# Segmented attention beside a gated MLP: filler of the score groups with three gate buffers, rings for K copies and Q chunks, and target periods

## The chip, the cores and the metric

The kernel runs on one core of one Trainium2 chip. The time is the device time of one launch in microseconds (us); all inputs and outputs lie in device memory. TensorE (PE) multiplies matrices into PSUM, VectorE (DVE) and ScalarE (ACT) read PSUM and SBUF, GpSimd (POOL) here only masks, SyncE (SP) issues DMAs.

## The reference

Both halves read the same x of shape 1 x 2048 x 512 in bf16. The first half is attention with a memory: 32 heads of width 16, the sequence cut into four segments of 512 rows.

```python
for s in range(4):
    logits = einsum('bhqd,bhkd->bhqk', qs, ks) * scale + mask     # causal inside the segment
    a_dot  = einsum('bhqk,bhkd->bhqd', softmax(logits), vs)
    a_mem  = (phi(qs) @ M) / (phi(qs) @ z + 1e-6)                 # phi(t) = t+1 for t>0, else exp(t)
    o      = g * a_mem + (1 - g) * a_dot                          # g = sigmoid(beta), one per head
    M, z   = M + phi(ks)^T vs, z + sum(phi(ks))
a = o @ wo
b = (gelu(x @ w_gate) * (x @ w_up)) @ w_down                      # 512 -> 1792 -> 512
out = sg * a + (1 - sg) * b                                       # sg = sigmoid(x . gate_w)
```

## The kernel before

All inputs are loaded once by SP in an order written by hand, and everything stays in SBUF. The x of each segment is held transposed (`xT`). The instruction order on every engine is written out by the program itself, at build time, by a small planner.

**Score groups.** The spine is a loop over four segments `s`, in each over four chunks `c` of eight heads, in each over five groups A to E: 80 groups in all, numbered by `clock`. `group_qk` writes the scores of one group into the single four-bank PSUM tile `lg` and ACT takes the exponential of it (`pT`). One group later `pv` multiplies the masked result by V (`od`). `finish` normalises on DVE (`rden`, `o2`). For s > 0 `mem_num` multiplies phi(q) by the memory (`mn`) and DVE scales it by `rdm`, which `u_den` computes. A finished chunk is transposed by a DMA into `oT` two groups later (`tr_o`).

**Filler.** Between a group's scores and its PV, PE is filled with units: `u_k`, `u_q`, `u_v` (projections of the next segment), `u_gate`, `u_up`, `u_down` (the MLP), `u_out` (the output), `u_M`, `u_den` (the memory). A projection, gate, up or output unit is four 512-wide matmuls into one of three general PSUM banks (`gen`) and one copy or product on DVE. `u_k` has two masked copies more, `KT`, for even and odd heads; `u_down` has 14 matmuls. Each unit carries an estimate of its PE and DVE time.

**Choice.** Units stand in streams, each in its own order: P (all projections and memory of one segment), G (gates), U (ups, then downs), O (outputs). `fill_to(t)` issues units until PE's planned time reaches `t`. It takes the first stream that has a unit allowed. If the planned backlog of DVE is over 0.5 us and the projections are not late against a linear pace, it takes the unit with the least DVE time per PE time:

```python
if backlog[0] > 0.5 and not late:
    st = min(hs, key=lambda x: x.q[0][1] / x.q[0][0])
start(st)
```

The feature maps phi (`u_phq`, `u_phk`) are issued by `later(lag, ...)`, some groups after their chunk. `u_absmax_x` and `u_bound` compute a bound on the scores that decides at the end whether a general path (not taken here) must run. The gate activations of a segment are copied to `G[s % 2]` and go through two large GELUs on ACT (`gelu`); for segment 0 ACT takes them straight out of PSUM in the opening.

**Buffers.** `G`, `QT` and `KTm` have two buffers each, taken by the segment's parity, so the gates of segment s wait for all downs of segment s-2, and all projections of a segment must be done before its first group.

Of the kernel before, what the change touches and what calls it, by code (L numbers as in the profile page):

```python
# [11 lines left out]
ALU = mybir.AluOpType  # L12
# [10 lines left out]
EXP_LIMIT = 80.0  # L23
BF = dt.bfloat16
# [11 lines left out]
TAIL_FILL = 5.5  # L36


@with_exitstack
def kernel(  # L40
# [188 lines left out]
    def u_q(s, c):  # L229
        def f():  # L230
            T = gen("qT")
            for fc in range(FC):
                nc.tensor.matmul(T[:, :], lhsT=wq[:, fc, c * P:(c + 1) * P],  # L233
                                 rhs=xT[:, fc, s * L:(s + 1) * L],
                                 start=(fc == 0), stop=(fc == FC - 1))
                if fc < FC - 1:
                    yield MM512
            nc.vector.tensor_copy(QT[s % 2][:, c, :], T[:, :])  # L238
            return MM512
        return 4 * MM512, EVAC, f  # L240
# [33 lines left out]
    def u_phq(s, c):  # L274
        def f():
            phi(pq[s % 2][:, c:c + 2, :], QT[s % 2][:, c:c + 2, :], ("q", s, c), 2 + c // 2)
        return 0.0, 0.0, f

    def u_phk(s, c):
        def f():  # L280
            phi(phk[:, c:c + 2, :], ktb[:, c:c + 2, :], ("k", s, c), 1 + c // 2)
        return 0.0, 0.0, f

    def u_k(s, c):
        def f():
            T = gen("kT")
            for fc in range(FC):
                nc.tensor.matmul(T[:, :], lhsT=wk[:, fc, c * P:(c + 1) * P],  # L288
                                 rhs=xT[:, fc, s * L:(s + 1) * L],
                                 start=(fc == 0), stop=(fc == FC - 1))  # L290
                if fc < FC - 1:
                    yield MM512
            nc.vector.tensor_copy(ktb[:, c, :], T[:, :])  # L293
            for p in range(2):
                nc.vector.tensor_scalar(out=KTm[s % 2][p][:, c, :], in0=ktb[:, c, :],  # L295
                                        scalar1=eo[:, p:p + 1], scalar2=None, op0=ALU.mult)
            return MM512
        return 4 * MM512, EVAC + 0.6, f
# [51 lines left out]
    def u_gate(s, hs, direct):  # L350
        def f():
            T = gen("gT")
            for fc in range(FC):
                nc.tensor.matmul(T[:, :], lhsT=wga[:, fc, hs * P:(hs + 1) * P],  # L354
                                 rhs=xT[:, fc, s * L:(s + 1) * L],
                                 start=(fc == 0), stop=(fc == FC - 1))
                if fc < FC - 1:
                    yield MM512
            if direct:
                nc.scalar.activation(G[s % 2][:, hs, :], T[:, :], AF.Gelu_apprx_tanh)  # L360
            else:
                nc.vector.tensor_copy(G[s % 2][:, hs, :], T[:, :])  # L362
            return MM512
        return 4 * MM512, EVAC, f

    def gelu(s):
        for h0 in range(0, HS, 7):
            g = G[s % 2][:, h0:h0 + 7, :]
            nc.scalar.activation(g, g, AF.Gelu_apprx_tanh)  # L369

    def u_up(s, hs):
        def f():
            T = gen("uT")
            for fc in range(FC):
                nc.tensor.matmul(T[:, :], lhsT=wup[:, fc, hs * P:(hs + 1) * P],  # L375
                                 rhs=xT[:, fc, s * L:(s + 1) * L],
                                 start=(fc == 0), stop=(fc == FC - 1))
                if fc < FC - 1:
                    yield MM512
            g = G[s % 2][:, hs, :]  # L380
            nc.vector.tensor_tensor(out=g, in0=T[:, :], in1=g, op=ALU.mult)  # L381
            return MM512
        return 4 * MM512, EVAC, f
# [3 lines left out]
    def u_down(s, qt):  # L387
        def f():
            T = gen("dT")
            for hs in range(HS):  # L390
                nc.tensor.matmul(T[:, :], lhsT=G[s % 2][:, hs, qt * P:(qt + 1) * P],  # L391
# [67 lines left out]
    def u_den(s):  # L459
        def f():  # L460
            assert ("q", s, 0) in ready and ("q", s, 2) in ready
            T = gen("zd")
            Tv = T[:, 0:KT * H].rearrange("p (q h) -> p q h", q=KT)
            for c in range(NC8):
                for qq in range(KT):
                    nc.tensor.matmul(Tv[:, qq, 8 * c:8 * c + 8],
                                     lhsT=pq[s % 2][:, c, qq * P:(qq + 1) * P],
                                     rhs=Mz[s % 2][:, c, :], start=True, stop=True)
                if c < NC8 - 1:
                    yield 0.12  # L470
            r = rdm[s % 2]
            nc.vector.tensor_scalar_add(r[:, :, :], Tv, 1e-6)
            nc.vector.reciprocal(r[:, :, :], r[:, :, :])
            nc.vector.tensor_tensor(out=r[:, :, :], in0=r[:, :, :],
                                    in1=gh[:, None, :].to_broadcast((P, KT, H)), op=ALU.mult)
            return 0.12
        return 0.5, 0.8, f
# [3 lines left out]
    def mem_num(s, c):  # L481
        assert count(("Mn", s)) > c // 2
# [13 lines left out]
    def group_qk(s, c, g):  # L496
# [8 lines left out]
        for pp, kt, off in pieces:  # L505
            n = L - kt * P
            for j in range(4):
                nc.tensor.matmul(lg[:, j, off:off + n],  # L508
                                 lhsT=KTm[s % 2][pp][32 * j:32 * j + 32, c, kt * P:(kt + 1) * P],
                                 rhs=QT[s % 2][32 * j:32 * j + 32, c, kt * P:L],  # L510
# [60 lines left out]

    class Stream:
        def __init__(self, name, units):
            self.name, self.q = name, deque(units)
            self.total = sum(u[0] for u in units)

    def unit(u, key=None, when=None):
        return u + (key, when)
# [55 lines left out]
    def fill_to(t):  # L634
        while True:
# [28 lines left out]
    for c in range(NC8):  # L664
        run(u_k(0, c))
# [5 lines left out]
    run(u_phk(0, 0))  # L671
    run(u_phk(0, 2))
# [19 lines left out]

    for s in range(NSEG - 1):
        us = []
        if True:
            now = (lambda s=s: clock[0] >= 20 * s + 2)
            us += [unit(u_pk(s, c), None,
                        lambda s=s, c=c: ("k", s, c - c % 2) in ready and clock[0] >= 20 * s + 2)
                   for c in range(NC8)]
            for c in range(NC8):  # L700
                us += [unit(u_k(s + 1, c), None, now), unit(u_q(s + 1, c))]
                if c % 2 == 1:
                    if s + 1 < NSEG - 1:
                        us.append(unit(u_phk(s + 1, c - 1)))
                    us.append(unit(u_phq(s + 1, c - 1)))
            us += [unit(u_v(s + 1, kt)) for kt in range(KT)]
            us += [unit(u_M(s, half)) for half in range(2)]
            us += [unit(u_mask(s + 1))]
            us.append(unit(u_den(s + 1), ("proj", s + 1),
                           lambda s=s: ("q", s + 1, 0) in ready and ("q", s + 1, 2) in ready))  # L710
            if s == 0:
                for i in range(NSEG):
                    us.insert(3 + 5 * i, unit(u_gate_logits(i)))
                us.insert(14, unit(u_absmax_x(2)))
                us.insert(19, unit(u_absmax_x(3)))
            if s == 1:
                us.insert(4, unit(u_bound()))
            streams.append(Stream("P", us))

    us = []  # L720
    for s in range(1, NSEG):
        us += [unit(u_gate(s, hs, False), None,
                    (lambda s=s: s < 2 or count(("down", s - 2)) == KT)) for hs in range(HS)]
        us.append(unit(u_gelu(s)))
    streams.append(Stream("G", us))

    us = []
    for s in range(NSEG):
        us += [unit(u_up(s, hs), None, lambda s=s: s == 0 or count(("gelu", s)) == 1)
               for hs in range(HS)]  # L730
        for qt in range(KT):
            us.append(unit(u_down(s, qt), ("down", s),
                           lambda s=s, qt=qt: count("gate") == 1
                           and (s == 0 or count(("out", s - 1)) > qt)))
# [44 lines left out]
    for s in range(NSEG):  # L779
        oT = wk2.tile([P, FC, L], BF, name="oT", tag="oT")  # L780
        oTs[s] = oT
        assert s == 0 or count(("proj", s)) == 1
        for c in range(NC8):
            for g in "ABCDE":
                clock[0] += 1
                t = group_qk(s, c, g)
# [51 lines left out]
    def general_blocks(s, c, p, tiles):  # L838
        spare = G[(s + 1) % 2]
# [5 lines left out]
        for qq in range(KT):  # L845
            n = (qq + 1) * P
            lg = plg.tile([P, 4, 512], F32, name="lg", tag="lg")
            for j in range(4):
                nc.tensor.matmul(lg[:, j, 0:n], lhsT=QT[s % 2][:, c, qq * P:n],
# [20 lines left out]
    def general():  # L870
# [3 lines left out]
        for s in range(NSEG):  # L874
# [7 lines left out]
            if s > 0:  # L882
                for c in range(0, NC8, 2):
                    phi_now(pq[s % 2][:, c:c + 2, :], QT[s % 2][:, c:c + 2, :])
                run(u_mask(s))
                run(u_den(s))
            neg = G[(s + 1) % 2][:, 8, 0:P]
# [70 lines left out]
```

## Time and profile before

| | us |
|---|---|
| median of three runs (297.51 to 299.5) | 299.48 |
| profiled execution | 299.61 |
| its span | 297.9 |
| PE busy | 280.0 (94%) |
| DVE busy | 214.1 (72%) |
| ACT busy | 200.8 (67%) |
| POOL busy | 83.4 (28%) |

The profile is of one execution. Times in its views count from the start of the span; what is beside the span in the run's time is 1.7 us. A line such as `PE gT L354 <- DVE QT L238: 2.2, 1, 2.2` says that PE, ahead of an instruction of line 354 that writes `gT`, sat idle until an instruction of DVE that writes `QT` was done: the sum in us, how often, and the longest. Rows of groups give the instruction's line, engine, operation, output and inputs, shapes and count, then its busy time, the mean of one in ns, and the idle time before. A matmul's duration includes its way through the array, so matmuls that follow each other overlap.

### The profile page before, as it was taken

To read this page: it belongs to the slowest core of one execution; us is meant where nothing else is said; L and a number is where in the kernel's file an instruction comes from. 1 tells how busy PE (TensorE), PEld (TensorE's weight loads), DVE (VectorE), ACT (ScalarE), POOL (GpSimd) and SP (SyncE) were. 2 spreads that over 40 slices of the span, in tenths; PEclk is the share of its full clock that TensorE was granted. 3 is DMA by queue.
4 is the path that set the end of the run, shared out by engine and by line. 5 is a ranking of instruction groups with operands and counts; after the bars stand their busy time and mean duration, and the time that the engine had idled before them with its cause. 6 is when DMAs were issued, how large, how long until landed. Compare 5 with 4: busy or idle time off the path is not lost. (4 is left out here: it accounts for less than half of the span.)

```text
span 297.9 us, 6858 instructions
## 1 busy us (share of the span) xinstructions
PE 280.0 (94%) x2910; PEld 138.4 (46%) x2960; DVE 214.1 (72%) x413; ACT 200.8 (67%) x125; POOL 83.4 (28%) x140
## 2 busy tenths in 40 slices
PE   7999999899999986999989999999999999999993
PEld 4444355454444443445445444455454454544551
DVE  1988698989945778678895396887886455775453
ACT  3236978698957768379976668677698666766600
POOL 4000134212243333130224433433401434244400
PEclk9999999999999999799999999999999999999998
DMA  6999850000023100000002141000000101001012
GB/s 215 319 266 212 294 74 20 0 2 20 0 20 72 21 2 19 2 10 10 0 2 55 28 80 37 3 18 2 20 0 19 36 20 37 0 21 37 21 39 77
DMA packets 29445, 15.86 MB, mean 53 GB/s; under 512 B 21984, under 2 KB 28384, under 8 KB 29408
## 3 DMA queue, kind: packets, MB, share of 16 engines
q1 hardware_dynamic: 29408, 15.35, 20.6%
q8 instruction: 25, 0.41, 0.6%
q14 instruction: 12, 0.10, 0.1%
HBM read 8.14 MB, written 2.10 MB: 34 GB/s over the span
## 5 line engine op out<-in xcount | busy, mean ns | idle before, releaser
L513 ACT ACTIVATE pT<-lg 128x2048 bf16<-128x2048 f32 x80 | 150.1, 1877 | 62.1 <-PE lg L508 52.2
L524 POOL TENSOR_SCALAR_AFFINE_SELECT pT<-pT 128x512 bf16<-128x512 bf16 x128 | 80.2, 644 | 198.9 <-ACT pT L513 197.0
L354 PE MATMUL gT<-xT,wga 128*128 128x512 bf16 x216 | 55.6, 388 | 4.7 <-DVE QT L238 2.2
L391 PE MATMUL dT<-wdn,G 128*128 128x512 bf16 x213 | 55.1, 380 | 0.9 <-issue 0.5
L375 PE MATMUL uT<-xT,wup 128*128 128x512 bf16 x211 | 51.9, 379 | 1.6 <-DVE G L381 0.8
L534 PEld LDWEIGHTS <-pT 128*128 128x128 bf16 x1280 | 43.6, 96 | 19.7 <-issue 2.6
L534 PE MATMUL od<-V,pT 128*128 128x17 bf16 x1280 | 44.0, 170 | 0.6 <-DVE o L544 0.4
L381 DVE TENSOR_TENSOR G<-uT,G 128x512 bf16<-128x512 f32 x56 | 37.7, 688 | 7.9 <-PE uT L375 7.8
L362 DVE CAST G<-gT 128x512 bf16<-128x512 f32 x42 | 28.0, 686 | 7.8 <-PE gT L354 7.2
L508 PE MATMUL lg<-QT,KT 32*128 32x384 bf16 (+3 forms) x512 | 31.7, 301 | 1.7 <-issue 1.1
L354 PEld LDWEIGHTS <-wga 128*128 128x128 bf16 x224 | 19.9, 98 | 27.9 <-issue 10.4
L375 PEld LDWEIGHTS <-wup 128*128 128x128 bf16 x224 | 19.5, 97 | 22.3 <-issue 3.9
L391 PEld LDWEIGHTS <-G 128*128 128x128 bf16 x224 | 18.5, 97 | 20.6 <-issue 5.0
L396 DVE TENSOR_SCALAR tB<-dT,omg 128x512 bf16<-128x512 f32 x16 | 12.0, 749 | 20.5 <-PE dT L391 20.4
L540 DVE RECIPROCAL rden<-od 128x16 f32<-128x16 f32 x32 | 8.2, 256 | 25.6 <-PE od L534 25.6
L508 PEld LDWEIGHTS <-KT 32*128 32x128 bf16 x512 | 9.0, 92 | 30.1 <-issue 29.6
L369 ACT ACTIVATE G<-G 128x3584 bf16<-128x3584 bf16 x6 | 18.8, 3182 | 0.0
L233 PE MATMUL qT<-xT,wq 128*128 128x512 bf16 x57 | 16.5, 380 | 0.8 <-DVE QT L238 0.2
L288 PE MATMUL kT<-xT,wk 128*128 128x512 bf16 x62 | 15.8, 379 | 0.6 <-issue 0.3
L360 ACT ACTIVATE G<-gT 128x512 bf16<-128x512 f32 x14 | 8.4, 598 | 11.3 <-PE gT L354 11.3
L408 PE MATMUL aT<-wo,oT 128*128 128x512 bf16 x58 | 15.6, 379 | 0.4 <-issue 0.2
L310 PE MATMUL vT<-wv,xT 128*128 128x512 bf16 x61 | 15.1, 379 | 0.1
(81 smaller groups left out, 222.8 us busy)
## 6 DMA issues: line engine op xcount, KB each, us to landing
out_dram<-osb SPq DMA_DIRECT2D x16, 128.0 KB, 1.7
wga<-in_B_w_gate_dram SPq DMA_DIRECT2D x1, 1792.0 KB, 12.4
wup<-in_B_w_up_dram SPq DMA_DIRECT2D x1, 1792.0 KB, 7.9
wdn<-in_B_w_down_dram SPq DMA_DIRECT2D x1, 1792.0 KB, 8.9
G<-in_A_x_dram SPq DMA_DIRECT2D x1, 512.0 KB, 4.1
wk<-in_A_wk_dram SPq DMA_DIRECT2D x1, 512.0 KB, 5.1
wq<-in_A_wq_dram SPq DMA_DIRECT2D x1, 512.0 KB, 5.9
wv<-in_A_wv_dram SPq DMA_DIRECT2D x1, 512.0 KB, 8.4
```

What stands on the lines that cost most here:

```text
L233: nc.tensor.matmul(T[:, :], lhsT=wq[:, fc, c * P:(c + 1) * P], rhs=xT[:, fc, s * L:(s + 1) * L], start=(fc == 0), stop=(fc == FC - 1))
L288: nc.tensor.matmul(T[:, :], lhsT=wk[:, fc, c * P:(c + 1) * P], rhs=xT[:, fc, s * L:(s + 1) * L], start=(fc == 0), stop=(fc == FC - 1))
L354: nc.tensor.matmul(T[:, :], lhsT=wga[:, fc, hs * P:(hs + 1) * P], rhs=xT[:, fc, s * L:(s + 1) * L], start=(fc == 0), stop=(fc == FC - 1))
L362: nc.vector.tensor_copy(G[s % 2][:, hs, :], T[:, :])
L369: nc.scalar.activation(g, g, AF.Gelu_apprx_tanh)
L375: nc.tensor.matmul(T[:, :], lhsT=wup[:, fc, hs * P:(hs + 1) * P], rhs=xT[:, fc, s * L:(s + 1) * L], start=(fc == 0), stop=(fc == FC - 1))
L381: nc.vector.tensor_tensor(out=g, in0=T[:, :], in1=g, op=ALU.mult)
L391: nc.tensor.matmul(T[:, :], lhsT=G[s % 2][:, hs, qt * P:(qt + 1) * P], rhs=wdn[:, hs, :], start=(hs == 0), stop=(hs == HS - 1))
L508: nc.tensor.matmul(lg[:, j, off:off + n], lhsT=KTm[s % 2][pp][32 * j:32 * j + 32, c, kt * P:(kt + 1) * P], rhs=QT[s % 2][32 * j:32 * j + 3 ...
L513: nc.scalar.activation(pT[:, :, :], lg[:, :, :], AF.Exp, scale=DH ** -0.5)
L524: nc.gpsimd.affine_select(out=v, in_=v, pattern=pat, compare_op=ALU.is_ge, fill=0.0, base=0, channel_multiplier=-1)
L534: nc.tensor.matmul(od[:, qq, j, 0:17], lhsT=t[:, j, o:o + P], rhs=V[s % 2][:, kt, 8 * c + 2 * j + p, 0:17], start=(kt == 0), stop=(kt == qq))
```

## The change

- `G` has three buffers, `G[s % 3]`: gates of segment s wait for the downs of segment s-3.
- `QT` has one buffer, in which a chunk is overwritten after its last score group. `KTm` is a ring of three chunks. So K and Q chunks of all segments form one sequence each, and a chunk may be issued once its place is free (`clock >= ...`).
- The opening computes three K chunks instead of four; the fourth is filler. The feature maps of k are filler from the start.
- The streams are eight instead of P, G, U, O: K, Q, V, M (transposes of phi(k), memory sums, denominators), Z (small parts), G, U, D (downs), O. Each unit has a target period `want`, a number of a group.
- `fill_to` takes the unit with the least target, where the target is shifted by DVE's backlog times the unit's DVE time per PE time.
- `need` issues what a group cannot do without, if it has not been issued.
- `u_den` is done for two chunks at a time, so its three small DVE operations run twice on half the width.
- The lags of the feature maps are the same for all chunks.

```diff
+NG = 3
+NK = 3
+WEIGH = 5.0
...
-    G = [const([P, HS, L], BF, f"G{i}") for i in range(2)]
-    QT = [const([P, NC8, L], BF, f"QT{i}") for i in range(2)]
-    KTm = [[const([P, NC8, L], BF, f"KT{p}{i}") for p in range(2)] for i in range(2)]
+    G = [const([P, HS, L], BF, f"G{i}") for i in range(NG)]
+    QT = const([P, NC8, L], BF, "QT")
+    KTm = [const([P, NK, L], BF, f"KT{p}") for p in range(2)]
...
-                nc.vector.tensor_scalar(out=KTm[s % 2][p][:, c, :], in0=ktb[:, c, :],
+                nc.vector.tensor_scalar(out=KTm[p][:, (NC8 * s + c) % NK, :], in0=ktb[:, c, :],
...
-    def u_den(s):
+    def u_den(s, pair):
...
-            for c in range(NC8):
+            for cc in range(2):
+                c = 2 * pair + cc
...
+            h0 = 16 * pair
+            r = rdm[s % 2][:, :, h0:h0 + 16]
+            nc.vector.tensor_scalar_add(r, Tv, 1e-6)
+            nc.vector.reciprocal(r, r)
...
-            st = hs[0]
-            if st.name == "P":
-                pace = st.total * (1.0 - ((clock[0] - 1) % 20) / 16.0)
-                late = sum(u[0] for u in st.q) > pace and backlog[0] < 1.5
-            else:
-                late = False
-            if backlog[0] > 0.5 and not late:
-                st = min(hs, key=lambda x: x.q[0][1] / x.q[0][0])
+            st = min(hs, key=lambda x: x.q[0][5] + WEIGH * x.q[0][1] / x.q[0][0] *
+                     (backlog[0] - 0.8))
             start(st)
...
-    for c in range(NC8):
+    for c in range(NK):
         run(u_k(0, c))
...
+    for i in range(NK, NSEG * NC8):
+        s, c = i // NC8, i % NC8
+        us.append(unit(u_k(s, c), 5 * i - 9, ("k", s),
+                       lambda i=i, s=s, c=c: clock[0] >= 5 * (i - NK) + 5 and
+                       (s == 0 or ("k", s - 1, c - c % 2) in ready)))
...
+    for i in range(NC8, NSEG * NC8):
+        s, c = i // NC8, i % NC8
+        us.append(unit(u_q(s, c), 5 * i - 11, ("q", s),
+                       lambda i=i: clock[0] >= 5 * (i - NC8) + 5))
...
+        us += [unit(u_v(s, kt), 20 * s - 13 + 3 * kt, ("v", s),
+                    lambda s=s: clock[0] >= 20 * s - 18) for kt in range(KT)]
...
+        us += [unit(u_M(s, half), 20 * s + 15) for half in range(2)]
+        us.append(unit(u_mask(s + 1), 0))
+        us += [unit(u_den(s + 1, pair), 20 * s + 18 + 10 * pair, ("den", s + 1),
+                    lambda s=s, pair=pair: ("q", s + 1, 2 * pair) in ready)
+               for pair in range(2)]
...
+    us = [unit(u_gate_logits(i), 3 + 3 * i) for i in range(NSEG)]
+    us += [unit(u_absmax_x(2), 14, None, lambda: clock[0] >= 14),
+           unit(u_absmax_x(3), 18, None, lambda: clock[0] >= 18),
+           unit(u_bound(), 45, None, lambda: clock[0] >= 45)]
...
+        us += [unit(u_gate(s, hs, False), 20 * (s - 1) + 1.1 * hs, None,
+                    lambda s=s: s < NG or count(("down", s - NG)) == KT) for hs in range(HS)]
...
+        step_ = 1.2 if s < NSEG - 1 else 0.6
+        us += [unit(u_up(s, hs), 20 * s + 1 + step_ * hs, ("up", s),
+                    lambda s=s: s == 0 or count(("gelu", s)) == 1) for hs in range(HS)]
...
+        first, step_ = ((18, 5), (38, 5), (58, 3), (70, 2.5))[s]
+        us += [unit(u_down(s, qt), first + step_ * qt, ("down", s),
...
-        us += [unit(u_out(s, qt), ("out", s),
+        us += [unit(u_out(s, qt), 20 * s + 24 + 4 * qt, ("out", s),
                     lambda s=s, qt=qt: count(("down", s)) > qt and count(("tr", s)) == NC8)
...
+    def need(key, n):
+        while count(key) < n:
+            if current:
+                step()
+            else:
+                heads()
+                start([st for st in streams if any(u[3] == key for u in st.q)][0])
```

More of the change, by code (lines that the diff above doesn't have):

```diff
@@ L280, in f @@
         def f():
-            phi(phk[:, c:c + 2, :], ktb[:, c:c + 2, :], ("k", s, c), 1 + c // 2)
+            phi(phk[:, c:c + 2, :], ktb[:, c:c + 2, :], ("k", s, c), 1)
         return 0.0, 0.0, f
@@ L574, in __init__, with unit @@
             self.name, self.q = name, deque(units)
-            self.total = sum(u[0] for u in units)
-    def unit(u, key=None, when=None):
-        return u + (key, when)
+    def unit(u, want, key=None, when=None):
+        return u + (key, when, want)
     streams = []
@@ L690, in u_gelu @@
         return 0.0, 0.0, f
[L693 to L718, printed above, removed]
@@ new lines, in free @@
+    def free(i):
+        return lambda: clock[0] >= 5 * (i - NK) + 5
+    us = [unit(u_phk(0, 0), 0)]
+    for i in range(NK, NSEG * NC8):
[3 more added lines that the diff above has]
+                       (s == 0 or ("k", s - 1, c - c % 2) in ready)))
+        if c % 2 == 1 and s < NSEG - 1:
+            us.append(unit(u_phk(s, c - 1), 0, None,
+                           lambda s=s: s == 0 or count(("pk", s - 1)) == NC8))
```

89 lines of the change are left out of this document (52 added, 37 removed).

## The prediction

> **What bounds the kernel now.** I read the page first (shares, clock row), then the waits summed by pair, then the time in stretches of 10 us, then the timeline at the worst stretch.
>
> ```profile
> PE 280.0 (94%) x2910; PEld 138.4 (46%) x2960; DVE 214.1 (72%) x413; ACT 200.8 (67%) x125; POOL 83.4 (28%) x140
> PEclk9999999999999999799999999999999999999998
> ACT pT L513 <- PE lg L508: 52.2, 54, 4.7
> PE gT L354 <- DVE QT L238: 2.2, 1, 2.2
> PE gT L354 <- DVE G L362: 1.0, 2, 0.8
> PE gT L354 <- DVE tm L489: 0.9, 1, 0.9
> PE uT L375 <- DVE G L381: 0.8, 1, 0.8
> PE od L534 <- DVE o L544: 0.4, 1, 0.4
> PE qT L233 <- DVE QT L238: 0.2, 1, 0.2
> PE qT L233 <- DVE ktb L293: 0.2, 1, 0.2
> ```
>
> TensorE (PE) sets the end: ScalarE (ACT) waits 52.2 us for it, and what PE itself waits for is nearly always VectorE (DVE). In the loop over the 80 score groups these waits are 2.2 + 1.0 + 0.9 + 0.8 + 0.4 = 5.3 us in six places, and 0.4 us more stand in the opening projections. The place matters:
>
> ```profile
> 100.00:110.00 10.00, 8.93 (x99) 4.34 (x100) 9.01 (x20) 6.76 (x4) 4.00 (x7) 1.00 0.07 15
> 110.00:120.00 10.00, 7.66 (x84) 3.52 (x83) 8.18 (x18) 7.41 (x5) 3.42 (x6) 0.94 0.07 14
> 120.00:130.00 10.00, 9.66 (x94) 4.46 (x94) 7.11 (x13) 4.82 (x3) 1.86 (x3) 0.89 0.01 2
> 230.00:240.00 10.00, 9.68 (x137) 5.07 (x135) 4.69 (x11) 6.71 (x5) 3.71 (x6) 1.00 0.14 38
> 115.36:118.77 3.41, 1.23 (x14) 0.44 (x12) 3.25 (x9) 2.96 (x3) 1.38 (x3) 1.00 0.20 41
> 118.77:122.18 3.41, 3.41 (x16) 1.31 (x16) 2.73 (x5) 0.00 (x0) 1.06 (x2) 0.50 0.00 0
> 116.16 0.40 PE L508 MATMUL lg<-QT,KT 32*128 32x256 bf16 x8
> 117.39 0.69 DVE L267 TENSOR_TENSOR phk<-phe,pha 128x1024 bf16<-128x1024 bf16 x1
> 118.00 0.68 DVE L238 CAST QT<-qT 128x512 bf16<-128x512 f32 x1
> 118.73 2.72 PE L354 MATMUL gT<-xT,wga 128*128 128x512 bf16 x6 [2.18 <-DVE QT L238]
> ```
>
> Columns of the stretches: length, busy time of PE, PEld, DVE, ACT, POOL, granted clock, DMA share, GB/s. Where projections, their copies and gate copies come together (100 to 130 us) DVE is 7 to 9 us busy of 10 and PE loses time; at 230 to 240 DVE has 4.69 us and PE runs through. At 116 us PE has nothing to do for 2.18 us because the copy of a Q chunk stands behind the feature map (L267) in DVE's order and all three general PSUM banks are full. Directly behind it the clock is 0.50 for 3.41 us, which costs 3.41 x 0.5 = 1.7 us.
>
> **The change, part by part.** PE's work is the same: the same number of matmuls of each kind stands in both programs. One K chunk (four matmuls) moves from the opening into the loop, which shifts 0.87 us and adds nothing. What changes is the order of the filler between score groups, so I count what each of the 80 groups issues in either program and multiply by these rows:
>
> ```profile
> 281.27 3.04 PE dT L391 x14
> 180.22 0.89 PE od L534 x36
> 193.68 0.25 PE MT L428 x4
> 156.81 0.33 PE lg L508 x8
> L381 DVE TENSOR_TENSOR G<-uT,G 128x512 bf16<-128x512 f32 x56 | 37.7, 688 | 7.9 <-PE uT L375 7.8
> L295 DVE TENSOR_SCALAR KT<-ktb,eo 128x512 bf16<-128x512 bf16 x32 | 12.2, 424 | 0.6
> L396 DVE TENSOR_SCALAR tB<-dT,omg 128x512 bf16<-128x512 f32 x16 | 12.0, 749 | 20.5 <-PE dT L391 20.4
> L540 DVE RECIPROCAL rden<-od 128x16 f32<-128x16 f32 x32 | 8.2, 256 | 25.6 <-PE od L534 25.6
> L541 DVE TENSOR_TENSOR rden<-rden,og 128x16 f32<-128x16 f32 x32 | 10.4, 325 | 1.1
> L544 DVE TENSOR_TENSOR o<-od,rden 128x256 bf16<-128x256 f32 x32 | 13.6, 424 | 1.1
> L762 DVE TENSOR_TENSOR o<-o,tm 128x512 bf16<-128x512 bf16 x12 | 5.1, 425 | 0.4
> L473 DVE RECIPROCAL rdm<-rdm 128x128 f32<-128x128 f32 x3 | 2.9, 953 | 0.1
> L206 DVE TENSOR_REDUCE bound<-bT x1: 534/534/534, 108.8 to 108.8; 1x3 f32<-1x384 f32 x1
> ```
>
> A 512-wide matmul is 3.04/14 = 0.217 us, a PV matmul 0.025, an M matmul 0.062, a group's scores 0.33. So a projection or gate unit is 0.87 us of PE and 0.69 of DVE, a K unit 0.69 + 2 x 0.42 = 1.54 of DVE, a down unit 3.04 of PE and 0.75 of DVE. The running sum "DVE work minus PE time, never below nothing" over the groups shows how far DVE is behind. With three banks, of which one is being written, PE can run two units ahead, 1.7 us.
>
> Before: in groups 7 to 10 DVE gets 13.9 us against 10.9 of PE, in 25 to 32 24.2 against 21.1. The sum is over 1.5 us in 17 of 80 groups, with 4.0 the highest; the waits above lie in or at the start of these stretches (51 to 55 us is group 8, 116 us group 28, 147 to 151 us group 35). After: Q and K chunks come one at a time over the whole segment and gate and up units are paired evenly; the sum is over 1.5 us in 5 groups (50 to 53, highest 2.3, where the three tiny tests of the bound, each as dear as the 0.53 us of the L206 row, meet a K chunk and a feature map; and 63 with 1.7), and 1.4 in group 20. So most of the stalls should go, not all: by the size of the present ones I keep 0.8 us at group 52 and 0.4 at 20 and 63, 1.6 us; bounds 0 and 4.2 (rivals below).
>
> The six waits of the loop are 5.3 us idle. A matmul counts as busy for 0.38 us though the next may start after 0.217, so each stall is 0.16 us longer than its idle time: 5.3 + 6 x 0.16 = 6.3 us. The slow clock goes with the 2.2 us stall: 1.7 us. The shorter opening (three K chunks, 1.5 us less DVE work ahead of the Q copies) takes its 0.4 us.
>
> The half clock is weighed against a rule by itself. The Trainium skill, "TensorE: Matmul & The Clock Gate", section on HAM oscillation, puts the fall to half rate at idle gaps over some 3.4 us; here 2.18 us of idle, in a stretch with 1.23 us busy of 3.41, preceded it. By the page that stall would be too short and the slow stretch would stay; by the row it goes. The result with it is the fourth case below.
>
> Three edits are costed at next to nothing. The third G buffer lets the gate of the next segment but one start early; no transfer or PE work is added. The division of `u_den` into two pairs turns three small operations into six of half size: between nothing and twice the 0.95 us of the reciprocal and its neighbours (0.28 and 0.29 us by their groups, not shown), I take 0.3 us of DVE per segment, which the running sum has in it. QT without a second buffer and KT as a ring of three make new chunks wait for old score matmuls; these stand ahead of the chunk's own matmuls on PE, and every copy is issued at least three groups, some 8 us, ahead of its first reader, so nothing is late. Up units now begin in group 1, at about 32 us; their weights are there:
>
> ```profile
> 16.30 0.51 SPq L114 DMA_DIRECT2D wup<-in_B_w_up_dram  x1
> 30.23 0.39 PE L508 MATMUL lg<-QT,KT 32*128 32x512 bf16 x4
> wup<-in_B_w_up_dram SPq DMA_DIRECT2D x1, 1792.0 KB, 7.9
> DMA to landing us min/median/max: 2.4/2.4/4.4
> ```
>
> 16.3 + 7.9 = 24.2 us. One step adds a wait. `u_out` has its own stream and target periods, and segment 0's first output unit now stands in group 23, close behind the transpose of that segment's last chunk (before: 16 groups after the segment's end; segments 1 and 2 keep five and nine groups in between). After the last PV matmul, in group 21, DVE has 0.6 to 1.1 us of K copies to end and 0.26 + 0.33 + 0.42 = 1.0 for the chunk; the transpose lands 2.4 later: 4.0 to 4.5 in all. PE has cover until the output unit's fourth matmul, the one that reads this chunk: 15 512-wide matmuls (3.3), two score groups (0.66), 4 PV (0.1), 4.0 us. So PE waits 0 to 0.5 us, up to 1.1 if already the unit's first matmul waits; all filler behind it waits too. I take 0.4.
>
> Sum against the profiled execution, 299.6 us (span 297.9 and 1.7 around it; the runs' median is 299.5, so nothing is to be converted): 299.6 - 6.3 - 1.7 - 0.4 + 1.6 + 0.4 = 293.2 us.
>
> **The rivals.**
>
> Cleaner than that: no stall is left at groups 20, 52 and 63, and the transpose is in time: 293.2 - 1.6 - 0.4 = 291.2. For it speaks that sums of 2.4 to 3.0 at groups 9 and 10 brought no listed wait; against it that group 45 with 1.0 did (the 0.4 us for `o`). ACT sets no bound close by: its waits for `lg` and for POOL's mask come to
>
> ```profile
> ACT pT L513 <- POOL pT L524: 9.7, 12, 1.1
> 104.44 1.88 ACT L513 ACTIVATE pT<-lg 128x2048 bf16<-128x2048 f32 x1 [0.64 <-PE lg L508]
> ```
>
> 61.9 us in 66 places; with 0.64 in each, what a prompt group shows, they would be 42, so ACT could end nearly 20 us sooner.
>
> The change does not do what it says: the picker weighs only the units' own copies, while feature maps, normalisations and bound tests fall on DVE by the clock of groups. Then two thirds of the 6.3 us stay, in new places (4.2 instead of 1.6), and with one wait near 2 us a slow stretch as well: 293.2 + 2.6 + 1.7 = 297.5. For it: DVE's work is the same to 2%. Against: the count by groups.
>
> The slow stretch stays for a reason of its own, the page's rule: 293.2 + 1.7 = 294.9.
>
> Slower: DVE becomes the bound of the whole stretch in which projections run. In groups 1 to 63 of the changed kernel it gets 165.7 us of work for 185.6 of PE, 0.89, with hardly a group in which it could catch up, and it must wait for each unit's last matmul before it can copy. If it works only 0.83 of the time there (8.18 of 10 us at 110 to 120 in the kernel before), the stretch takes 165.7 / 0.83 = 199.6: 14.0 more, in place of the 1.6 kept, 305.6. It decides from a share under 0.89 on, and makes the kernel slower by 1% at 165.7 / 196.5 = 0.84. Against it:
>
> ```profile
> 70.00:80.00 10.00, 9.79 (x101) 4.45 (x102) 9.36 (x20) 8.55 (x8) 3.71 (x6) 1.00 0.01 2
> ```
>
> where DVE is busy 9.36 of 10 us and PE hardly loses any.
>
> **How the numbers follow.** Forecast 293.2: 0.50, with 291.3 to 295.3 as its own spread. Cleaner, 291.2: 0.15. Slow stretch stays, 294.9: 0.10. Two thirds of the stalls stay, 297.5: 0.15. DVE as the bound, 305.6: 0.07. Something else slower: 0.03. Faster by over 1%, about what a measurement of this kernel can tell from no change (its runs spread by 0.7%), means below 296.5: the first three and 0.02 of the fourth, 0.77. Within 1%: 0.14. Slower: 0.09. The range goes from the cleaner case with the opening another microsecond better, 290.0, to a little over the fourth case, 298.3; outside lie DVE as the bound and the tails.
>
> **What would show it.** Right: the waits of PE for DVE in the loop sum to 1 to 2 us with none over 1; no stretch at clock 0.50 between 6 us and the end of the matmuls; DVE in the 10 us stretches up to 230 us between 6.5 and 9.2; the first score matmul near 29 us and the span near 291.5; a short wait of PE `aT` for the transpose at about 95 us. Wrong: PE stalls of 1 us or more for QT, KT or `tm` copies, `lg` waiting for KT or QT, up units waiting for their weights at 32 us, or ACT's waits for `lg` shrunk to 0.64 each while PE waits for ACT.

## The result, and the profile after

The changed kernel took 295.71 us (295.11 to 296.18, four runs) beside 298.5 of the kernel before (297.39 to 299.5, four runs): ratio 0.9893, 95% interval 0.9849 to 0.9938, 2.8 us or 1.1% faster. The forecast was 293.2 with 290.0 to 298.3.

One thing must be known to read any ratio below: the kernel before took 299.1 to 300.3 us at a mean granted clock of 0.991 to 0.994 in 36 of the 58 runs that later experiments shared, and 297.4 to 298.1 us at 0.996 to 1.0 in the other 22. The profiled execution, 299.61 us, is one of the 36 and shows what sets them apart: the stretch at clock 0.50. All four runs of the changed kernel had 0.997 to 0.999. Against the 22, some 297.7, the change is worth 2.0 us, and the ranges do not touch.

The page and the waits of the changed kernel (profiled execution 295.11, span 293.3):

```profile
PE 283.3 (97%) x2960; PEld 138.3 (47%) x2960; DVE 215.6 (74%) x422; ACT 200.8 (68%) x125; POOL 83.4 (28%) x140
PEclk9999999999999999999999999999999999999999
ACT pT L525 <- PE lg L519: 45.2, 49, 2.4
PE dT L397 <- DVE G L387: 1.3, 2, 1.1
PE uT L381 <- DVE G L387: 1.0, 1, 1.0
PE uT L381 <- DVE G L368: 0.2, 1, 0.2
```

The 5.3 us of the loop's six waits for VectorE (DVE) have become 2.5, and two waits, 1.1 and 1.0, hold most of that. The clock row has no dip, and ScalarE (ACT) still waits 45.2 us for the scores, so TensorE (PE) still sets the end. PE's busy totals are not to be compared: of PE's 2960 matmuls the trace of before holds 2910. Stretches of 10 us:

```profile
70.00:80.00 10.00, 8.90 (x96) 4.76 (x94) 7.59 (x17) 9.36 (x6) 1.86 (x3) 1.00 0.06 13
100.00:110.00 10.00, 9.86 (x102) 4.52 (x95) 7.58 (x13) 7.01 (x5) 3.96 (x7) 1.00 0.05 16
110.00:120.00 10.00, 10.00 (x145) 5.44 (x144) 9.44 (x22) 7.50 (x6) 3.71 (x6) 1.00 0.22 50
120.00:130.00 10.00, 10.00 (x111) 4.65 (x109) 7.31 (x14) 7.39 (x4) 3.30 (x6) 1.00 0.24 46
140.00:150.00 10.00, 9.21 (x103) 4.84 (x102) 8.15 (x19) 8.47 (x6) 3.08 (x5) 1.00 0.06 13
230.00:240.00 10.00, 10.00 (x99) 4.94 (x98) 7.63 (x14) 7.84 (x5) 1.85 (x3) 1.00 0.01 2
```

From 110 to 120 us, where PE had lost most, it now loses nothing, with DVE busier than before (9.44 of 10 us). The loss sits at 70 to 80 and at 140 to 150. The timeline at the first place:

```profile
73.33 0.42 DVE L556 TENSOR_TENSOR o<-od,rden 128x256 bf16<-128x256 f32 x1
73.47 1.03 PE L316 MATMUL vT<-wv,xT 128*128 128x512 bf16 x4
73.67 0.68 DVE L185 TENSOR_REDUCE amax<-xT 128x1 f32<-128x512 bf16 x1
74.26 0.42 DVE L271 TENSOR_SCALAR pha<-QT 128x1024 bf16<-128x1024 bf16 x1
74.34 1.03 PE L381 MATMUL uT<-xT,wup 128*128 128x512 bf16 x4
74.79 0.69 DVE L273 TENSOR_TENSOR pq<-phe,pha 128x1024 bf16<-128x1024 bf16 x1
74.82 6.27 ACT L375 ACTIVATE G<-G 128x3584 bf16<-128x3584 bf16 x2
75.40 0.42 DVE L446 TENSOR_TENSOR Mn<-Macc,bm 128x256 bf16<-128x256 f32 x1
75.73 0.68 DVE L387 TENSOR_TENSOR G<-uT,G 128x512 bf16<-128x512 f32 x1
76.47 1.89 PE L397 MATMUL dT<-wdn,G 128*128 128x512 bf16 x8 [1.10 <-DVE G L387]
```

Here ACT is taken by the large GELU (6.27 us), so the planner puts a long row of filler between two score groups. In front of it DVE has five small operations (o, amax, pha, pq, Mn) ahead of the product that frees a PSUM bank (75.73); the banks are full and PE stands still for 1.10 us. At 148.8 us the second GELU does the same with another set of small operations.

Where the span's 4.6 us came from, by the first and last PE rows of each part:

| | before | after | difference |
|---|---|---|---|
| first K matmul | 6.93 | 6.20 | -0.73 |
| to the first score matmul | 23.30 | 22.05 | -1.25 |
| to the last chunk's transpose on PE | 257.62 | 254.39 | -3.23 |
| to the end of the span | 10.03 | 10.67 | +0.64 |

The K chunk moved 0.87 us from the second row into the third, and three matmuls of a down unit (0.65) from the third into the fourth. Without moved work the opening became 0.4 us shorter and the loop 3.45, of which 1.7 is the half-clock stretch; the other 1.75 is put down to waits. The first row can't be put down to the change: in the profiles of the experiments, most with this same opening, the first K matmul starts anywhere from 6.13 to 7.08 us, so two runs can differ by almost 1 us before the first K chunk. In experiments 1, 2 and 5 the opening also waited 0.8 to 1.8 us for the DMA of `wq`; where it did not, it took 22.05 to 22.07 us with three K chunks and 23.30 to 23.32 with four.

### The profile page after: what moved, and what is told of

Read it like the earlier page. It is cut to its first block, busy times and chain, and to the rows that moved or that the text cites. A ratio compares the mean times of both kernels' runs of the same rounds, so it can differ in the third digit from the quotient of the medians.

```text
span 293.3 us, 6911 instructions
## 1 busy us (share of the span) xinstructions
PE 283.3 (97%) x2960; PEld 138.3 (47%) x2960; DVE 215.6 (74%) x422; ACT 200.8 (68%) x125; POOL 83.4 (28%) x140
## 4 chain that ended last, share of the span: by engine, by line
PE 86%; DVE 11%; issue 1%; ACT 1%; DVEq 0%
PE dT L397 17%; PE gT L360 16%; PE uT L381 16%; PE od L546 10%; PE lg L519 8%; PE kT L294 4%; PE vT L316 4%; PE aT L414 4%; PE qT L239 4%; DVE ktb L299 1%; PE warm L147 1%; DVE tm L500 1%; DVE KT L301 1%; DVE rden L553 1%; DVE o L556 1%
## 5 line engine op out<-in xcount | busy, mean ns | idle before, releaser
L525 ACT ACTIVATE pT<-lg 128x2048 bf16<-128x2048 f32 x80 | 150.1, 1876 | 59.7 <-PE lg L519 45.2
L381 PE MATMUL uT<-xT,wup 128*128 128x512 bf16 x224 | 62.2, 380 | 1.4 <-DVE G L387 1.0
L360 PE MATMUL gT<-xT,wga 128*128 128x512 bf16 x224 | 59.3, 379 | 0.4
L368 DVE CAST G<-gT 128x512 bf16<-128x512 f32 x42 | 28.8, 686 | 6.6 <-PE gT L360 6.3
L397 PEld LDWEIGHTS <-G 128*128 128x128 bf16 x224 | 19.8, 97 | 24.0 <-issue 4.8
L239 PE MATMUL qT<-xT,wq 128*128 128x512 bf16 x64 | 17.1, 378 | 0.2
L294 PE MATMUL kT<-xT,wk 128*128 128x512 bf16 x64 | 17.3, 379 | 0.1
L316 PE MATMUL vT<-wv,xT 128*128 128x512 bf16 x64 | 17.0, 380 | 0.0
L414 PE MATMUL aT<-wo,oT 128*128 128x512 bf16 x64 | 16.3, 380 | 0.0
L299 DVE CAST ktb<-kT 128x512 bf16<-128x512 f32 x16 | 11.0, 690 | 5.3 <-PE kT L294 5.1
```

The lines of the kernel that those rows point to most:

```text
L316: nc.tensor.matmul(T[:, :], lhsT=xT[:, fc, s * L + kt * P:s * L + (kt + 1) * P], rhs=wv[:, fc, :], start=(fc == 0), stop=(fc == FC - 1))
L368: nc.vector.tensor_copy(G[s % NG][:, hs, :], T[:, :])
L397: nc.tensor.matmul(T[:, :], lhsT=G[s % NG][:, hs, qt * P:(qt + 1) * P], rhs=wdn[:, hs, :], start=(hs == 0), stop=(hs == HS - 1))
L525: nc.scalar.activation(pT[:, :, :], lg[:, :, :], AF.Exp, scale=DH ** -0.5)
```

## The experiments

"Full clock" means a run without the half-clock stretch. All medians stand beside runs of the kernel before on the same chip, whose medians were 299.35 to 299.58.

**1. The stall at 116 us, and the half clock.** The kernel before, with the bound test one segment later:

```diff
-            if s == 1:
+            if s == 2:
                 us.insert(4, unit(u_bound()))
```

> The kernel before, with the three tests of the bound (`u_bound`) issued among the projections of segment 3 instead of segment 2, nothing else. Theory (the stall of 2.2 us at 116 us comes from DVE being late, and the stretch at clock 0.50 behind it comes from that stall): the stall falls under 1 us, no stretch at clock 0.50 stands before the end of the matmuls, and the time is 299.5 - 2 - 1.7 = 295.8 us, 295.3 to 297. Rival (the slow stretch has a cause of its own, as the Trainium skill's rule of 3.4 us of idleness would have it): the stall goes, a slow stretch stays, 297.5.

297.89 us (297.33 to 298.09, ten runs), ratio 0.9958 (0.9934 to 0.9983). The clock was 0.996 to 1.0 in all ten, where 36 of 58 runs of the kernel before have the stretch. The time forecast by the theory, 295.8, was missed. The 2.2 us wait is gone, but the waits came up elsewhere:

```profile
PE gT L354 <- DVE G L362: 1.7, 2, 0.9
PE gT L354 <- DVE QT L238: 0.7, 1, 0.7
PE MT L428 <- DVE V L314: 0.6, 1, 0.6
PE uT L375 <- DVE G L362: 0.5, 1, 0.5
PE uT L375 <- DVE tm L489: 0.4, 1, 0.4
PE od L534 <- DVE o L544: 0.4, 1, 0.4
```

So the half clock goes when the one long stall goes. The stall's own 2.2 us did not go: the time is that of the kernel before at full clock, and the loop, 255.8 us, is before's 257.6 less the 1.7 of the stretch.

**2. The third gate buffer**, in the changed kernel: `NG = 2` instead of 3.

> The changed kernel with two gate buffers instead of three, so gates of segment s again wait for the downs of segment s-2. Theory (the gain is the spreading of DVE work by targets and backlog, for which the third buffer is hardly needed): the running sum of DVE work against PE time stays under 1.6 us in all groups, and the time is 295.0 to 296.5 against 295.7 of the changed kernel. Rival (the gates that run ahead in the third buffer are what keeps PE fed): 297.5 or more, with PE waits at the segment ends.

295.49 us (295.21 to 296.37, four runs), ratio 0.9887 (0.9834 to 0.9939). The waits at the two GELUs are still 1.1 and 1.0. The theory holds: the third buffer is worth nothing that can be measured.

**3. The picker's weight**, in the changed kernel: `WEIGH = 0.0` instead of 5.0, so that target periods alone decide between the streams (nine of them: K, Q, V, M, Z, G, U, D, O).

> The changed kernel with WEIGH = 0: units are picked by their target periods alone, DVE's backlog has no say. The running sum is then over 1.5 us in 13 groups (18 to 28, 49, 50) instead of 5. Theory (the shift by backlog is a part of the gain): 1.5 to 3 us of PE waits for DVE more, 297 to 299. Rival (targets alone spread the work, the weight is idle): 295.7 within 0.5.

302.04 us (301.77 to 302.12, four runs), ratio 1.0106 (1.0053 to 1.0159): 6.3 us slower than with the weight, slower than before, and 3 us more than the theory's upper end. The clock row, and the timeline where it falls:

```profile
PEclk9999999999989999999999999999999999999999
84.23 0.40 PE L519 MATMUL lg<-QT,KT 32*128 32x256 bf16 x8
84.34 0.69 DVE L368 CAST G<-gT 128x512 bf16<-128x512 f32 x1 [0.17 <-PE gT L360]
84.95 0.68 DVE L185 TENSOR_REDUCE amax<-xT 128x1 f32<-128x512 bf16 x1
85.54 0.42 DVE L271 TENSOR_SCALAR pha<-QT 128x1024 bf16<-128x1024 bf16 x1
86.06 0.69 DVE L273 TENSOR_TENSOR pq<-phe,pha 128x1024 bf16<-128x1024 bf16 x1
86.81 0.35 PE L473 MATMUL zd<-Mz,pq 128*128 128x8 bf16 x8 [2.18 <-DVE pq L273]
84.13:87.54 3.41, 1.23 (x20) 0.61 (x20) 2.99 (x8) 3.41 (x3) 1.86 (x3) 1.00 0.00 0
87.54:90.95 3.41, 3.41 (x20) 1.09 (x18) 3.01 (x6) 0.03 (x1) 0.63 (x2) 0.50 0.00 0
```

Again a stall of 2.18 us, by another wait in another place, PE busy 1.23 us in the 3.41 around it, and behind it 3.41 us at clock 0.50, which is 1.7 of the 6.3 us. All four runs had 0.992 or 0.993.

**4. Absolute maxima and bound test moved** to groups 64 to 78, where no projections run:

```diff
-    us += [unit(u_absmax_x(2), 14, None, lambda: clock[0] >= 14),
-           unit(u_absmax_x(3), 18, None, lambda: clock[0] >= 18),
-           unit(u_bound(), 45, None, lambda: clock[0] >= 45)]
+    us += [unit(u_absmax_x(2), 64, None, lambda: clock[0] >= 64),
+           unit(u_absmax_x(3), 68, None, lambda: clock[0] >= 68),
+           unit(u_bound(), 73, None, lambda: clock[0] >= 73)]
```

> The changed kernel with the eight absmax reductions of x (0.68 us of DVE each, groups 15 to 22) and the bound tests (group 45 on) moved to groups 64 to 78, where DVE has little to do. Theory (the 1.1 us wait of PE for G at 76 us, and the one at 150 us, come from small DVE work issued ahead of the bank-freeing copies at the start of the GELU groups 17 and 40): the wait at group 17 loses some 0.7 us, the one at group 40 stays, and 294.6 to 295.4. Rival (these waits are set by something else, the ups' order): 295.7 and the same two waits of 1.1 and 1.0.

294.79 us (294.53 to 295.91, four runs), ratio 0.9879 (0.9823 to 0.9934). The wait at the first GELU, where an amax stood in DVE's row, falls from 1.10 to 0.55; at the second, where none stood, it stays, as the theory has it. The medians differ by 0.9 us, but the ranges overlap, so the two waits say more than the time:

```profile
76.56 1.02 PE L381 MATMUL uT<-xT,wup 128*128 128x512 bf16 x4 [0.55 <-DVE Macc L440]
149.86 1.02 PE L381 MATMUL uT<-xT,wup 128*128 128x512 bf16 x4 [1.04 <-DVE G L387]
```

**5. Up units closer together**: the kernel of experiment 4 with one up unit every 1.1 groups instead of 1.2.

> The kernel of e4_absmax_late with the ups' target step 1.1 instead of 1.2, so that at the GELU groups all ups of the segment are done and a down unit (14 matmuls, one DVE operation) can stand first. Theory (the two waits at the start of the GELU groups come from up and V units whose copies queue behind 3.6 us of small DVE work there): both waits fall under 0.3 us and the time is 1.0 to 1.5 us under that of e4_absmax_late, 293.3 to 294.0. Rival (DVE is late there whatever the units' order, the wait only moves to the next unit): 294.8 within 0.4.

293.87 us (292.79 to 294.19, six runs), ratio 0.9817 (0.9779 to 0.9854). The time is as the theory has it. Of the two waits, none is left at the second GELU, but 0.6 us stays near the first, and a new one of 1.0 us stands at 260.7 (`uT` for `osb`).

**6. Only the shorter opening**, on the kernel before with its own picker and buffers:

```diff
-    for c in range(NC8):
+    for c in range(NC8 - 1):
         run(u_k(0, c))
...
-    run(u_phk(0, 2))
...
             if s == 0:
+                us = [unit(u_k(0, 3)), unit(u_phk(0, 2))] + us
```

> The kernel before with one part of the change alone: three K chunks in the opening, the fourth (with its feature map) as the first filler. Theory (the opening loses one K unit's 0.87 us, which the loop gets, and 0.4 us of waits): the first score matmul comes 1.2 us earlier, and the time is 0.4 us under that of the kernel before at the same clock. Rival (the 1.5 us of DVE work that moves into groups 1 to 16, where the running sum is highest, comes back as PE waits): first score matmul 1.2 us earlier, time equal or up to 1 us longer.

295.82 us (295.45 to 296.01, six runs), ratio 0.9891 (0.9854 to 0.9927), which is the time of the whole change, and full clock in all six. This was not expected by either theory. The opening itself gave the 0.4 us again. The rest came in the loop, where the longest waits are 1.0 and 0.9 us, and experiments 8, 9 and 11 ask whether it belongs to the edit.

**7. The weight as well**: experiment 4 with an up unit every 1.15 groups and `WEIGH = 4.0`.

> The kernel of e4_absmax_late with the ups' step 1.15 and WEIGH 4, which by the order of instructions puts the GELU one group ahead of the Q feature map and of the masking of the memory in segments 0 and 1, so that the GELU groups 17 and 40 get 7.6 and 8.5 us of DVE work instead of 10.4 and 12.0, but still begin with up and V units. Theory (it is the small DVE work at the start of these groups that makes the waits): both waits fall under 0.4 us as in e5_ups_earlier, 293.5 to 294.2. Rival (only a unit without copies at the start helps): one or both waits of 1 us stay, 294.8.

292.31 us (291.72 to 293.04, six runs), ratio 0.9776 (0.9739 to 0.9814). It beats both kernels and lies below what its theory forecast (293.5); as two settings changed at once, no run divides the gain between them. All waits of PE for DVE in the loop that its trace lists, and the stretches that were worst before:

```profile
PE gT L360 <- DVE G L368: 0.4, 1, 0.4
PE qT L239 <- DVE QT L244: 0.2, 1, 0.2
100.00:110.00 10.00, 10.00 (x134) 5.16 (x133) 6.84 (x13) 7.67 (x5) 3.67 (x6) 1.00 0.05 15
110.00:120.00 10.00, 10.00 (x110) 4.92 (x111) 9.67 (x22) 8.15 (x5) 3.15 (x6) 1.00 0.35 76
120.00:130.00 10.00, 10.00 (x113) 4.66 (x112) 7.83 (x15) 7.00 (x5) 4.29 (x7) 1.00 0.18 31
```

(The `qT` wait is in the opening.) DVE is busy 9.67 of 10 us and PE loses nothing.

**8. Four K chunks in the opening**, in the changed kernel with two gate buffers: `NK = 4`, and both feature maps of k first in the filler.

```diff
-    us = [unit(u_phk(0, 0), 0)]
+    us = [unit(u_phk(0, 0), 0), unit(u_phk(0, 2), 0)]
```

> The changed kernel with four K chunks in the opening, as before the change; to have room, G has two buffers (which cost nothing in e2_two_G) and the K ring four chunks. Theory A (the parts add: the shorter opening is worth 1.2 us, of which the moved unit gives 0.87 back): 295.7 + 0.4 = 296.1, first score matmul at 29.5 to 30.3 us. Theory B (e6_three_K_before shows nearly the whole gain to come from the opening): 297.5, as the kernel before at full clock. Theory C (both are ways to the same thing, an order of the loop that has no long stall, and either does it): 295.5 to 296.3, no wait of PE over 1.3 us in the loop and no slow stretch.

298.01 us (296.85 to 299.01, twelve runs), ratio 0.9971 (0.9946 to 0.9995): 2.5 us over experiment 2, and no better than the kernel before at full clock. Theory B comes nearest; that the parts add (A) is out, and so is C. PE stalls longest at 38.7 us, 1.5 us longer from start to start than a matmul needs; experiment 11 shows by what.

**9. Experiments 1 and 6 together**, on the kernel before.

> The kernel before with three K chunks in the opening and the bound tests among the projections of segment 3, so two small edits and the old picker. Theory A (the edits add: e6_three_K_before's waits of 1.0 and 1.2 us at 106 and 114 us stand where the bound tests are, and go with them): 294.3 to 295.0. Theory C (the old picker keeps DVE late in some place, the wait moves): 295.4 to 296.2.

297.68 us (296.58 to 298.28, twelve runs), ratio 0.9954 (0.9931 to 0.9978). Two edits, one worth 1.9 us and one that took away the half clock, do not add up: the opening is that of experiment 6, and the median is 1.9 us over it, outside both theories. The longest waits stand in new places:

```profile
PE uT L375 <- DVE G L381: 1.5, 2, 1.3
PE gT L354 <- DVE QT L238: 1.2, 1, 1.2
```

Between the two profiled executions the loop is 1.2 us longer (256.42 beside 255.25), and 0.7 us more is a later first K matmul (7.08 beside 6.37), which can't be put down to the edit. So with the old picker only the opening's 0.4 us is sure to belong to the three chunks; the rest of experiment 6's 1.9 hangs on the order of the loop and is nearly lost when that order shifts.

**10. Is experiment 7 a lucky order?** The same with `WEIGH = 3.0`.

> A near neighbour of e7_phi_off_gelu, WEIGH 3 instead of 4, nothing else. If e7's 292.3 us comes from the place of its GELU groups, this one, whose GELU of segment 1 stands one group later (group 41, 9.6 us of DVE work), should be 292.0 to 293.2. If e7 was a lucky alignment, up to 1.5 us over it.

292.09 us (291.8 to 292.93, six runs), ratio 0.9784 (0.975 to 0.9817). The neighbour is as fast, and its waits for DVE in the loop are 0.5 us and less. Between weight 3 and 4, then, the time does not depend on one order.

**11. Four K chunks with the settings of experiment 7.**

> The kernel with four K chunks in the opening (ring of four, two gate buffers, 298.01) with the three settings of the best version so far (absolute maxima and bound test in groups 64 to 78, up units every 1.15 groups, weight 4). Theory A, the loss of 2.3 us against its three-chunk sister is the place of stalls that each re-shuffle moves: with the settings that leave no stall it comes to 292.3 + 0.4 = 292.7, the 0.4 being DVE's extra feature map and copies in the opening (span from the first K matmul to the first gate matmul 11.1 us instead of 9.9, of which 0.87 is the chunk itself). Theory B, three K chunks in the opening and the shorter ring are themselves worth 2.3: 294.6, with stalls of about 1 us at groups 2 to 4 in which the chunks' feature maps meet the gate copies.

294.87 us (294.44 to 295.83, six runs), ratio 0.9864 (0.9827 to 0.99), 2.6 us over experiment 7. The theory that the settings would leave only 0.4 (A) falls; the time and the place of the stall are those of theory B. The timeline at the largest stall:

```profile
36.97 0.67 DVE L271 TENSOR_SCALAR pha<-ktb 128x1024 bf16<-128x1024 bf16 x1
37.74 0.69 DVE L273 TENSOR_TENSOR phk<-phe,pha 128x1024 bf16<-128x1024 bf16 x1
38.46 0.43 DVE L271 TENSOR_SCALAR pha<-ktb 128x1024 bf16<-128x1024 bf16 x1
38.99 0.69 DVE L273 TENSOR_TENSOR phk<-phe,pha 128x1024 bf16<-128x1024 bf16 x1
39.60 0.68 DVE L368 CAST G<-gT 128x512 bf16<-128x512 f32 x1
40.34 1.02 PE L381 MATMUL uT<-xT,wup 128*128 128x512 bf16 x4 [1.32 <-DVE G L368]
```

With four chunks done in the opening both feature maps of k come together at the start of the loop, ahead of the gate copy; with three the second follows later. Between the profiled executions of experiments 7 and 11 the opening without the moved chunk grows by 0.4 us and the loop by 3.0, while the first K matmul comes 0.7 sooner. Of the loop's 3.0 this stall is 1.5 (start to start); most of the rest are waits of 1.0 us for `osb` at 260.9 and 0.5 for `V`. The one for `osb` stands in experiment 5 too, with three chunks, so it is not owed to the fourth. Whether four chunks with the second feature map put later would do as well as three was not run.

**12. The old picker with the tests moved**: experiment 6 with absolute maxima and bound test in groups 64 to 78, as in experiment 4.

> The kernel before with three K chunks in the opening (295.82) and the absolute maxima and the bound test moved to groups 64 to 78, where no projections run; picker, buffers and streams as before. Theory A, what the picker weighs matters and the old one only moves its stalls: 295 to 297.5, with the same 1.5 to 3 us of waits for VectorE in other places. Theory B, the tests are what VectorE is late by, whatever the picker: 293.5 or less, waits under 1 us in all, and the change's picker would not be needed.

294.48 us (293.94 to 295.17, six runs), ratio 0.9845 (0.981 to 0.9881), between the two theories: moving the tests gives 1.3 us, and a stall of 1.02 us for `QT` at 114.5 us and one of 0.6 for `V` stay where feature map, K and Q copies meet.

The medians side by side (us; the kernel before at full clock):

| | tests in their place | tests in groups 64 to 78 | also spacing 1.15, weight 4 |
|---|---|---|---|
| old picker, four K chunks in the opening | 297.7 | | |
| old picker, three | 295.8 | 294.5 | |
| new picker, four (two gate buffers) | 298.0 | | 294.9 |
| new picker, three (the change) | 295.7 | 294.8 | 292.3 |

## Why the prediction was right, and where it was off

The sign, the range and the bound were right: PE still sets the end, and what went is PE's waiting for DVE and the half clock behind one of these waits. But 295.71 lies outside the 291.3 to 295.3 that the forecast gave as its own spread. Against the profiled executions, 299.61 and 295.11, the forecast was 6.4 us and the drop 4.5, of which 0.73 is the earlier first K matmul, for which the prediction has no reason. Without the half clock, in the runs at full clock, the forecast's other terms come to 4.7 us, and the change gave 2.0.

*The half-clock stretch, 1.7.* Right in size, and in cause as far as the runs show. It went with the 2.2 us stall in experiment 1, where nothing but one test was moved, and came back in experiment 3 with another stall of 2.18 us. By the Trainium skill, "TensorE: Matmul & The Clock Gate", section on HAM oscillation, it is PE-idle gaps over some 3.4 us that are to be avoided. Here 2.18 us were enough, so the measurement decides, and the rival built on that rule (294.9, because the stretch would stay) is out, though the time came near it. What the prediction did not see is that the stretch is there in only some of the runs of before, so this term counts in the profile and only in part in a median; its "nothing is to be converted" took 299.5 for the usual time.

*The opening, 0.4.* Right: 23.30 to 22.05 us less the 0.87 moved, and the same in every experiment whose opening did not wait for a DMA.

*The six waits, 6.3, less 1.6 and 0.4 kept.* This is the mis-sized term: they gave 1.75, not 4.3, and the sign named for it, 1 to 2 us of waits with none over 1, was missed with 2.5 us and one of 1.1. The six places themselves were cleared, and the stretch from 100 to 130 us came out as forecast. Wrong was where stalls would remain. No listed wait stands in group 20 or 50 to 53 and only 0.17 us in 63, the groups in which the running sum was highest; the two large ones stand at the GELUs, in groups 17 and 40, which are not among them. At groups 50 to 53 one price was also too high: the three small tests of the bound, taken at 0.53 us each, took 0.14 to 0.15 each in the changed kernel (185.7 to 186.1 us). The sum treats a group as one lump, and a group with a GELU holds many microseconds of filler, so it looked like slack. What counts is DVE's order inside it: the small operations at its start stand ahead of the copies that free banks. Experiment 4 shows it by taking one of them out (1.10 to 0.55), and experiments 7 and 10, with both places clear, agree. What the listed waits do not hold of the shortfall is in short gaps, by a comparison with experiment 7: its loop is 4.2 us shorter (250.16 beside 254.39), of which the two GELU stalls, at 0.16 us over their idle time each, are 2.5, and no other is over 0.5.

Which part of the change made the gain at full clock is shown only in part. Three chunks in the opening, put alone into the kernel before, reach the time of the whole change (experiment 6), and the change with four is no faster than the kernel before at full clock (experiment 8). So the even spread by targets and backlog, the prediction's reason, did not carry the gain by itself.

*The output unit behind the transpose, 0.4.* Wrong: no wait.

```profile
L414 PE MATMUL aT<-wo,oT 128*128 128x512 bf16 x64 | 16.3, 380 | 0.0
DMA to landing us min/median/max: 2.4/2.4/3.3
```

The transposes (`oT`, second row) land as fast as before, and the cover of 4.0 us was enough.

*The third gate buffer at nothing.* Right, by experiment 2.

*DVE as the bound* did not come. In the 10 us stretches from 10 to 230 us it was 6.4 to 9.4 busy; 9.44 and, in experiment 7, 9.67 went without loss.

*"The change doesn't do what it says"*, two thirds of the stalls stay. It named the right mechanism: small operations issued by the clock of groups are what the picker cannot place. By the 1.75 us measured, some 4.5 of the 6.3 stayed, where this rival had 4.2, but without a long stall and so without its slow stretch; its sum without the 1.7 is 295.8, which is what was measured. So the forecast's own case gave the number less well than this one. Experiment 3 shows that the weight on the backlog does work, 6.3 us of it with the half clock; experiments 6 and 12 show that the same targets with that weight, as set in the change, were no better than the old picker with a shorter opening. With the tests out of the way and the two settings of experiment 7, the new picker is 2.2 us faster than the old one with the same opening and tests (292.3 against 294.5).

Open is how much of experiment 6's loop gain comes from the first filler unit and how much from later places. With the old picker it does not last under another order (experiment 9); with the new one the fourth chunk in the opening costs 2.5 and 2.6 us under two orders (experiments 8 and 11), of which the opening's 0.4 and the stall of 1.5 behind the feature maps are accounted for.

## What to carry to other kernels

When an engine in front is held by one that frees its buffers, look at the order of that engine's queue inside each stretch, not at sums of work: 9.67 of 10 us busy cost nothing here, and five small operations in one place cost 1.1 us. Work that has no due time (tests, maxima) belongs where its engine has no copies to make, and removing a stall by moving one unit must be tried with neighbouring settings, since a stall often only moves. A single profile can hold an event that only some runs have: compare its clock with that of the other runs before taking it as a term.

## What the runs showed of the hardware

A single idle time of PE of 2.2 us was followed by 3.41 us at clock 0.50: in the profiles of before and of experiment 3, and by time and mean clock in 36 of 58 runs of the kernel before (some 2 us each) and in all four of experiment 3. No profile in which the longest stall in the loop was 1.3 us or less shows it.

Why the same stall brings it in one run and not in the next was not tested, but the traces offer a reason. In each trace the clock records begin and change at times that are whole multiples of 3.41 us apart (before: 6.13, 118.77, 122.18, 296.26; experiment 3: 5.62, 87.54, 90.95, 299.17), and where this grid lies against the kernel differs from trace to trace. Cut along their grids from the first record to the last change, the fourteen traces hold 1177 stretches of 3.41 us. In 16 of them PE was busy 1.3 us or less, the two stalls (1.23 each) and fourteen at the ends of the programs, and the half clock followed each. In all others PE was busy 1.65 us or more, and it followed none. The two nearest to the limit, from experiments 12 and 2, with the half clock behind the first alone:

```profile
286.72:290.13 3.41, 1.30 (x7) 0.39 (x4) 1.87 (x3) 0.00 (x0) 0.00 (x0) 1.00 0.47 156
8.97:12.38 3.41, 1.65 (x9) 0.60 (x7) 2.65 (x8) 0.77 (x2) 0.00 (x0) 1.00 1.01 382
```

So in these traces it is not the length of the gap alone that counts but how busy PE is in one stretch of the grid, and a stall of 2.18 us that falls across a line of the grid leaves more busy time on either side of it. If the grid lies by chance, the stall would bring the half clock in 40 to 61% of the runs, by a limit of 1.3 or of 1.65 us (an estimate: 1.23 of the 3.41 us in which a line can fall leave the stall whole, and 0.07 to 0.42 at either side leave enough of it); it was 36 of 58, or 62%. All four runs of experiment 3 would then be a chance of at most one in seven.
